# A hint ahead of the general path's branch, weight sums in place over four steps, and separate buffers for the first pair's token sums

## The chip, the cores and the metric

The kernel runs on one core of a Trainium2 chip. Its engines are PE (matrix products; PEld is the loading of weights into it), DVE, ACT and POOL (elementwise work), and SP, which here only issues DMAs. The metric is the time of one execution in device microseconds (us), as the median of three runs: 838.96 us before the change (838.41 to 841.43).

## The reference

```python
for t in range(S):                                  # S = 768, state is 48 x 48 for each of 4 x 8 heads
    kt, vt, rt = (k[:, :, t], v[:, :, t], r[:, :, t])
    cur = np.einsum('bhd,bhe->bhde', u[None] * kt, vt)
    y[:, :, t] = np.einsum('bhd,bhde->bhe', rt, state + cur)
    state = w[None, :, :, None] * state + np.einsum('bhd,bhe->bhde', kt, vt)
x = y.transpose(0, 2, 1, 3).reshape(3072, 384)      # tokens by model width
h = x @ w_in                                        # 384 -> 2048
x = (np.maximum(h, 0.0) + alpha * np.minimum(h, 0.0)) @ w_out   # 2048 -> 384
a, b = x @ w1, x @ w2                               # 384 -> 1024, both
out = (a * b @ w3) @ w_out2                         # 1024 -> 1024 -> 384
```

All is f32 in and out.

## The kernel before

The work runs over six blocks of 128 time steps (all four batches together: 512 tokens). Inside a block the recurrence is done in chunk form for four pairs of heads (a pair is a unit): scores (`sc`, L292), the masked copy of them into `am` (DVE, L305 and L308) and the outputs `py` (L351, L357). The outputs are the `x` of the next block's first layer, so the units of block i+1 and the layer of block i are interleaved. A block's first layer has 16 steps f: `product1` (PE, `ph`, nine matmuls, one of two PSUM banks by the parity of f), `relus` (ACT, L583 and L584), `slope` (DVE, L589), `halves` (ACT and POOL, `gh` and `gl`) and, three steps behind, `down1` (PE, `acc`, nine matmuls). Every f32 product is made of three matmuls on a high and a low half of both operands; `split` makes the halves (ACT casts the high, POOL subtracts for the low).

The second layer multiplies w3 by w_out2 first (`fold`: 24 matmuls into `pf`, for each of eight j), so that its end is one product with `m`. Its two first products are done for two blocks at once, a pair of blocks p = 0, 1, 2, in the seven products of Strassen's form as rearranged here. This wants sums of weights (the **mix**: b = w11-w10, e = b+w01, a = e-w00, p = w01+w11) and sums of tokens (`x_sum`). The second layer's weights were split during the earlier blocks and lie in DRAM (`s12`, `so2`, `s3`).

The order on each engine is that in which the program calls things: a written schedule (`MIDDLE`, a list of words for every four steps, and `LAST` for the last block) names the calls of each step. In the fifth block (i == NB-2) an even step ends with `mix_store` of the former weight slice and `mix_load` of the next, an odd step with `mix`, the sums and the split. All engines are in-order queues, SP too. SP gives each DMA one of eight semaphores in turn, and a DMA waits until the one that had the same semaphore has landed.

In the last block `extra` (the word `xx`) starts what the second layer needs: two `w3` slices at the block's start (`fetch_3`), the weights by step (`fetch_12`), the eight `so2` slices (`fetch_o2`), a `fold` in each of the steps 4 to 11, the loads of `x2d` and the first sums of tokens. Fold j+2's `w3` is loaded right behind fold j, into the two buffers of tags `rk` and `nat`. The first sums of tokens, at steps 6 and 7, take their buffer from the tag `rk` too. The first four `so2` slices use the four buffers of the tag `raw`, which the mix uses as well. The group f of a pair in `second` is 42 matmuls of the seven products with 18 of the output product between them.

At the end stands `tc.If(flag > 0)` over `general()`, the path for weights w out of a range. The data here never take it, so every engine branches over its code (L1128), waits once for its semaphores in the short block behind it, and passes the final barrier (L1209).

## Time and profile before

| | |
|---|---|
| median of three runs | 838.96 us |
| the profiled execution | 837.99 us |
| its span, first to last instruction | 836.2 us |
| mean granted clock of PE | 0.995 of full speed |
| busy PE, DVE, POOL, ACT | 97%, 63%, 51%, 43% |
| DMA traffic | 139.5 MB, 167 GB/s in the mean |

The page gives the busy time of each engine, and the span in 40 slices. A timeline lists instructions in order: start, length, engine, line, operation, output and inputs, sizes, and in brackets the idle time in front of it and what ended that. A q behind an engine's name is its sequencer, which issues DMAs, waits and branches. Waits are summed by waiter and by what it waited for.

### The profile page before, as it was taken

To read this page: it belongs to the slowest core of one execution; us is meant where nothing else is said; L and a number is where in the kernel's file an instruction comes from. 1 tells how busy PE (TensorE), PEld (TensorE's weight loads), DVE (VectorE), ACT (ScalarE), POOL (GpSimd) and SP (SyncE) were. 2 spreads that over 40 slices of the span, in tenths; PEclk is the share of its full clock that TensorE was granted. 3 is DMA by queue.
4 is the path that set the end of the run, shared out by engine and by line. 5 is a ranking of instruction groups with operands and counts; after the bars stand their busy time and mean duration, and the time that the engine had idled before them with its cause. 6 is when DMAs were issued, how large, how long until landed. Compare 5 with 4: busy or idle time off the path is not lost.

```text
span 836.2 us, 13560 instructions
## 1 busy us (share of the span) xinstructions
PE 814.5 (97%) x4910; PEld 669.9 (80%) x4910; DVE 529.6 (63%) x880; ACT 355.7 (43%) x703; POOL 422.6 (51%) x342
## 2 busy tenths in 40 slices
PE   8999999999999999999889999999999999999995
PEld 7777788888888888888778898888887888888884
DVE  5899998988787887766654121154467445674442
ACT  3587666555555565543345232432223222331221
POOL 3778876766677667655654122342244223432221
PEclk9999999999999999999999999999999999999999
DMA  8666765766677677655539735325332453342002
GB/s 251 181 205 188 201 216 163 253 211 236 211 222 229 179 232 197 191 161 154 158 121 313 286 127 205 101 94 185 118 109 100 151 189 114 106 160 76 1 0 81
DMA packets 63247, 139.52 MB, mean 167 GB/s; under 512 B 7169, under 2 KB 24066, under 8 KB 63170
## 3 DMA queue, kind: packets, MB, share of 16 engines
q1 hardware_dynamic: 62338, 137.24, 52.0%
q10 hardware_dynamic: 832, 1.31, 0.5%
q8 instruction: 41, 0.67, 0.3%
q14 instruction: 36, 0.29, 0.1%
HBM read 104.15 MB, written 31.46 MB: 162 GB/s over the span
## 4 chain that ended last, share of the span: by engine, by line
PE 77%; DMA 7%; DVE 5%; issue 3%; POOL 3%; ACT 2%; SPq 2%; DVEq 0%; POOLq 0%; ACTq 0%
PE pq L753 21%; PE acc L124 8%; PE acc L125 7%; PE acc L126 7%; PE ph L124 6%; PE ph L125 6%; PE ph L126 6%; PE py L357 2%; PE py L351 2%; PE acb L126 2%; PE acb L124 2%; PE acb L125 2%; DMA mix<-s 2%; DMA wo<-so 1%; PE pf L125 1%
## 5 line engine op out<-in xcount | busy, mean ns | idle before, releaser
L121 POOL TENSOR_TENSOR gl<-g,gh 128x512 fp32r<-128x512 f32 x96 | 126.5, 1318 | 118.2 <-ACT gh L120 115.2
L121 POOL TENSOR_TENSOR gl<-t,gh 128x512 fp32r<-128x512 f32 x48 | 72.1, 1509 | 169.4 <-PE pq L753 145.3
L764 DVE TENSOR_TENSOR t<-pq,t 128x512 f32<-128x512 f32 x96 | 66.2, 689 | 97.4 <-PE pq L753 97.4
L124 PE MATMUL ph<-x,wi 128*128 128x512 f32 x288 | 115.5, 401 | 4.3 <-ACT p L584 3.1
L589 DVE SCALAR_TENSOR_TENSOR g<-g,keep,p 128x512 f32<-128x512 f32 x80 | 78.6, 983 | 61.5 <-ACT p L584 58.1
L124 PE MATMUL acc<-gh,wo 128*128 128x512 f32 x288 | 114.4, 397 | 0.0
L125 PE MATMUL ph<-x,wi 128*128 128x512 f32 x288 | 113.1, 393 | 1.2 <-POOL wi L150 1.2
L126 PE MATMUL ph<-x,wi 128*128 128x512 f32 x288 | 112.5, 390 | 0.0
L125 PE MATMUL acc<-gh,wo 128*128 128x512 f32 x288 | 112.3, 390 | 0.0
L126 PE MATMUL acc<-gl,wo 128*128 128x512 f32 x288 | 112.3, 390 | 0.0
L753 PE MATMUL pq<-x,w 128*128 128x512 f32 x408 | 110.8, 390 | 0.0
L753 PE MATMUL pq<-xc,w 128*128 128x512 f32 x384 | 107.1, 391 | 0.0
L120 ACT CAST gh<-t 128x512 fp32r<-128x512 f32 x48 | 29.9, 623 | 140.3 <-DVE t L764 140.3
L753 PEld LDWEIGHTS pq<-x,w 128*128 128x128 f32 x408 | 76.6, 188 | 16.1 <-DVE t L764 0.2
L753 PEld LDWEIGHTS pq<-xc,w 128*128 128x128 f32 x384 | 72.0, 188 | 15.8 <-DVE xc L708 0.6
L120 ACT CAST gh<-g 128x512 fp32r<-128x512 f32 x96 | 59.2, 619 | 52.8 <-DVE g L589 51.9
L583 ACT ACTIVATE g<-ph 128x512 f32<-128x512 f32 x96 | 56.9, 593 | 37.4 <-PE ph L126 35.3
L124 PEld LDWEIGHTS ph<-x,wi 128*128 128x128 f32 x288 | 54.1, 188 | 18.7 <-ACT p L584 4.3
L124 PEld LDWEIGHTS acc<-gh,wo 128*128 128x128 f32 x288 | 54.1, 188 | 12.5 <-issue 1.1
L125 PEld LDWEIGHTS ph<-x,wi 128*128 128x128 f32 x288 | 54.1, 188 | 12.4 <-POOL wi L150 2.2
L126 PEld LDWEIGHTS ph<-x,wi 128*128 128x128 f32 x288 | 54.1, 188 | 11.5
L126 PEld LDWEIGHTS acc<-gl,wo 128*128 128x128 f32 x288 | 54.1, 188 | 11.3
(138 smaller groups left out, 1482.8 us busy)
## 6 DMA issues: line engine op xcount, KB each, us to landing
w<-s SPq DMA_DIRECT2D x72, 384.0 KB, 4.4
raw<-in_wA SPq DMA_DIRECT2D x32, 384.0 KB, 3.8
s<-raw SPq DMA_DIRECT2D x32, 384.0 KB, 4.1
nat<-in_nat SPq DMA_DIRECT2D x20, 576.0 KB, 7.1
rk<-in_rkT SPq DMA_DIRECT2D x20, 448.0 KB, 6.5
raw<-in_wB SPq DMA_DIRECT2D x16, 384.0 KB, 5.1
raw<-in_w3T SPq DMA_DIRECT2D x16, 384.0 KB, 4.2
x2d<-o SPq DMA_DIRECT2D x18, 256.0 KB, 2.1
```

The lines of the kernel that those rows point to most:

```text
L120: nc.scalar.copy(out=dst_h, in_=src)
L121: (lo or nc.gpsimd).tensor_tensor(out=dst_l, in0=src, in1=dst_h.bitcast(F32), op=ALU.subtract)
L124: nc.tensor.matmul(out=o, lhsT=wh, rhs=xh, start=first, stop=False)
L125: nc.tensor.matmul(out=o, lhsT=wl, rhs=xh, start=False, stop=False)
L126: nc.tensor.matmul(out=o, lhsT=wh, rhs=xl, start=False, stop=last)
L351: nc.tensor.matmul(out=py[o:e, b], lhsT=state[:, hp, b, o:e], rhs=t["rs"][:, b], start=b == 0, stop=False, skip_group_check=True,)
L357: nc.tensor.matmul(out=py[o:e, b], lhsT=t["v"][:, b, D * j:D * j + e - o], rhs=t["am"][:, B * j + b], start=i == 0 and b == 0, stop=True, ...
L583: nc.scalar.activation(out=g, in_=ph, func=ACTF.Relu, scale=-1.0)
L589: nc.vector.scalar_tensor_tensor(out=g, in0=g, scalar=alpha[:, f:f + 1], in1=p, op0=ALU.mult, op1=ALU.add)
L753: nc.tensor.matmul(out=o, lhsT=u, rhs=v, start=first and n == 0, stop=last and n == 2, skip_group_check=True)
L764: nc.vector.tensor_tensor(out=o, in0=x, in1=y, op=how)
```

## The change

- **The hint.** `second(True)` marks a place ahead of the last group for a branch hint with the label of the branch over `general()`, on all engines.
- **The mix.** The sums are now made in the buffers that the loads filled (two tiles instead of six for a slice): `mix` makes the sums in the first half of each tile, the new `mix_split` puts the high halves into the second and the low ones into the first, and `mix_store` writes them back in six DMAs instead of four. `mix_step` runs the four in four successive steps: load at an even step, sums in the odd one behind it, the split in the even one behind that, the store in the next odd one. The last slice so runs into the first two steps of the last block. In the stored layout b and a change places, and `where` in `group` follows.
- **The `so2` loads.** In the last block slices 4 to 7 are issued ahead of the first `fetch_12`, and slices 0 to 3 at step 2 instead of step 1.
- **The token sums.** The first two sums of the first pair take buffers of the tag `o` in the pool `gp`, not of `rk`.

```diff
--- before.py
+++ after.py
@@ -463,24 +463,32 @@
             nc.sync.dma_start(out=parts[j], in_=seen(f, j, 0, 2))
 
     def mix(f):
-        parts = mixes[f]
-        t, o = (st.tile([P, 4, P], F32, tag="raw", name="mix") for _ in range(2))
         op = nc.vector.tensor_tensor
-        for j in range(2):
-            op(out=t[:, 2 * j:2 * j + 2], in0=parts[j][:, 0], in1=parts[j][:, 1], op=ALU.add)
-        w00, w01, w10, w11 = (t[:, m] for m in range(4))
-        op(out=o[:, 0], in0=w11, in1=w10, op=ALU.subtract)
-        op(out=o[:, 1], in0=o[:, 0], in1=w01, op=ALU.add)
-        op(out=o[:, 2], in0=o[:, 1], in1=w00, op=ALU.subtract)
-        op(out=o[:, 3], in0=w01, in1=w11, op=ALU.add)
-        mixes[f] = h, l = [st.tile([P, 4, P], F32R, tag="raw", name="mix") for _ in range(2)]
-        split(h, l, o)
+        for x in mixes[f]:
+            op(out=x[:, 0], in0=x[:, 0], in1=x[:, 1], op=ALU.add)
+        (w00, w01), (w10, w11) = ((x[:, 0, 0], x[:, 0, 1]) for x in mixes[f])
+        op(out=w10, in0=w11, in1=w10, op=ALU.subtract)
+        op(out=w11, in0=w11, in1=w01, op=ALU.add)
+        op(out=w01, in0=w10, in1=w01, op=ALU.add)
+        op(out=w00, in0=w01, in1=w00, op=ALU.subtract)
+
+    def mix_split(f):
+        for x in mixes[f]:
+            nc.scalar.copy(out=x[:, 1].bitcast(F32R), in_=x[:, 0])
+            nc.gpsimd.tensor_tensor(out=x[:, 0].bitcast(F32R), in0=x[:, 0], in1=x[:, 1], op=ALU.subtract)
 
     def mix_store(f):
-        for s, x in enumerate(mixes.pop(f)):
-            x = x.bitcast(F32)
-            nc.sync.dma_start(out=seen(f, 2, 0, KD)[:, s], in_=x[:, 0:KD])
-            nc.sync.dma_start(out=seen(f, 1, 1, 2)[:, s], in_=x[:, KD:])
+        ae, bp = mixes.pop(f)
+        for s in range(2):
+            nc.sync.dma_start(out=seen(f, 2, 0, 2)[:, s], in_=ae[:, 1 - s])
+            nc.sync.dma_start(out=seen(f, 2, 2, 3)[:, s], in_=bp[:, 1 - s, 0:1])
+            nc.sync.dma_start(out=seen(f, 1, 1, 2)[:, s], in_=bp[:, 1 - s, 1:2])
+
+    def mix_step(k):
+        for fn, n in ((mix_store, 3), (mix_split, 2), (mix, 1), (mix_load, 0)):
+            f, odd = divmod(k - n, 2)
+            if not odd and 0 <= f < M2:
+                fn(f)
 
     def fetch_o2(k):
         if k < 5:
@@ -683,10 +691,12 @@
 
     def x_sum(p, name):
         k = NAMES.index(name)
-        if k in (1, 3, 5):
-            xt2[p, k] = ld.tile([P, 2, N], F32, tag="rk", name="xsum")
-        s = xt2[p, k] if k in (1, 3, 5) else xt2[p, k - 1]
-        s = s[:, k in (2, 4)]
+        if p == 0 and k < 3:
+            s = gp.tile([P, N], F32, tag="o", name="xsum", bufs=3)
+        else:
+            if k in (1, 3, 5):
+                xt2[p, k] = ld.tile([P, 2, N], F32, tag="rk", name="xsum")
+            s = (xt2[p, k] if k in (1, 3, 5) else xt2[p, k - 1])[:, k in (2, 4)]
         xs[p, name, "sum"] = s
         if name[0] == "-":
             nc.vector.scalar_tensor_tensor(
@@ -743,7 +753,7 @@
 
     def group(p, f, after):
         w = [w2s[3 * (M2 * p + f) + m] for m in range(3)]
-        where = {"w00": (0, 0), "w01": (0, 1), "w02": (0, 2), "w10": (1, 0), "p": (1, 1), "w12": (1, 2), "b": (2, 0), "e": (2, 1), "a": (2, 2)}
+        where = {"w00": (0, 0), "w01": (0, 1), "w02": (0, 2), "w10": (1, 0), "p": (1, 1), "w12": (1, 2), "a": (2, 0), "e": (2, 1), "b": (2, 2)}
 
         def times(o, name, x, first, last=True):
             m, c = where[name]
@@ -822,7 +832,7 @@
         after(8)
         pull()
 
-    def second():
+    def second(hint=False):
         for k in range(NB // 2 * M2):
             p, f = divmod(k, M2)
 
@@ -856,6 +866,8 @@
                             x_low(p + 1, "x21", nc.vector)
                             x_cast(p + 1, "x20")
 
+            if hint and k == NB // 2 * M2 - 1:
+                tc.mark_branch_hint_location("rare", engines=mybir.ALL_ENGINES)
             if f == 3 and p + 1 < NB // 2:
                 load_x2(p + 1)
             group(p, f, after)
@@ -1045,11 +1057,9 @@
 
         def extra(x):
             f = x % M1
-            if f == 0:
-                mix_store(M2 - 1)
+            for k in {0: (4, 5, 6, 7), 2: (0, 1, 2, 3)}.get(f, ()):
+                fetch_o2(k)
             fetch_12(f)
-            for k in ((4, 5, 6, 7), (0, 1, 2, 3))[f] if f < 2 else ():
-                fetch_o2(k)
             if f == 2:
                 late[0] = True
             j = f - 4
@@ -1109,13 +1119,8 @@
                         table[name](x - k)
                 else:
                     table[name](x)
-            if i == NB - 2:
-                if f % 2:
-                    mix(f // 2)
-                else:
-                    if f:
-                        mix_store(f // 2 - 1)
-                    mix_load(f // 2)
+            if i >= NB - 2:
+                mix_step(x - M1 * (NB - 2))
         if STOP:
             return
         table["hl"](NB * M1 - 1)
@@ -1123,9 +1128,9 @@
             for c in range(KD):
                 queue.append(lambda f=f, c=c: down(NB - 1, f, wo[f], M1, x2d, (c,)))
         pull()
-        second()
+        second(True)
     flag = nc.values_load(rare, min_val=0, max_val=1)
-    with tc.If(flag > 0):
+    with tc.If(flag > 0, label="rare"):
         general()
```

How this moves instructions: on ACT in the fifth block (steps 4 to 7 of it; `gh` is the cast of a step's product, `g` and `p` its two relus, `x` the outputs of a unit). Before:

```order
L120 CAST gh<-g 128x512
L583 ACTIVATE g<-ph 128x512
L584 ACTIVATE p<-ph 128x512
L120 CAST mix<-mix 128x512
L120 CAST gh<-g 128x512
L394 CAST x<-py 112x512
L583 ACTIVATE g<-ph 128x512
L584 ACTIVATE p<-ph 128x512
L120 CAST gh<-g 128x512
L583 ACTIVATE g<-ph 128x512
L584 ACTIVATE p<-ph 128x512
```

and now:

```order
L477 CAST mix<-mix 128x256 x2
L120 CAST gh<-g 128x512
L591 ACTIVATE g<-ph 128x512
L592 ACTIVATE p<-ph 128x512
L120 CAST gh<-g 128x512
L394 CAST x<-py 112x512
L591 ACTIVATE g<-ph 128x512
L592 ACTIVATE p<-ph 128x512
L477 CAST mix<-mix 128x256 x2
L120 CAST gh<-g 128x512
L591 ACTIVATE g<-ph 128x512
```

The cast of the mix stood in front of a step's casts and relus, directly behind the sums; now its two halves stand behind the relus of a step in which the sums are a step old.

On SP at the same place (`x<-e` moves a unit's outputs and waits for them, `mix<-s` is the load of the next slice, `s<-mix` the store; `rk` and `nat` are the inputs of a later unit). Before:

```order
L366 DMA x<-e 16x2x512 x2
L482 DMA s_108<-mix 128x384
L483 DMA s_108<-mix 128x128
L482 DMA s_108<-mix 128x384
L483 DMA s_108<-mix 128x128
L463 DMA mix<-s_108 128x2x256 x2
L173 DMA rk<-in_rkT 112x1024
L174 DMA nat<-in_nat 128x1152
```

and now:

```order
L366 DMA x<-e 16x2x512 x2
L463 DMA mix<-s_108 128x2x256 x2
L483 DMA s_108<-mix 128x256
L484 DMA s_108<-mix 128x128
L485 DMA s_108<-mix 128x128
L483 DMA s_108<-mix 128x256
L484 DMA s_108<-mix 128x128
L485 DMA s_108<-mix 128x128
L173 DMA rk<-in_rkT 112x1024
L174 DMA nat<-in_nat 128x1152
```

The load stood behind four stores of the slice before; now it stands ahead of them, right behind the move of the outputs.

On SP in the steps 1 to 2 of the last block (`wo<-so` are `so2` slices, `x2d<-o` the first layer's results of the fifth block, `w` the weights of the second layer). Before:

```order
L453 DMA w_1_5220<-s_108 128x768
L488 DMA wo_5222<-so_109 128x768
L488 DMA wo_5224<-so_109 128x768
L488 DMA wo_5226<-so_109 128x768
L488 DMA wo_5228<-so_109 128x768
L626 DMA x2d<-o 128x512 x3
L453 DMA w_2_5267<-s_108 128x768
```

and now:

```order
L453 DMA w_1_5214<-s_108 128x768
L483 DMA s_108<-mix 128x256
L484 DMA s_108<-mix 128x128
L485 DMA s_108<-mix 128x128
L483 DMA s_108<-mix 128x256
L484 DMA s_108<-mix 128x128
L485 DMA s_108<-mix 128x128
L634 DMA x2d<-o 128x512 x3
L496 DMA wo_5259<-so_109 128x768
L496 DMA wo_5261<-so_109 128x768
L496 DMA wo_5263<-so_109 128x768
L496 DMA wo_5265<-so_109 128x768
L453 DMA w_2_5267<-s_108 128x768
```

The four `so2` slices 0 to 3 now stand behind the last stores of the mix and the three stores of results.

The hint, on SP, at the top of the program (PE, ACT, DVE and POOL have it as the first instruction behind the branch into the kernel as well):

```order
L1214 UNCONDITIONAL_BRANCH
L1214 BRANCH_PREFETCH_HINT
L1003 DMA wu<-in_wu 112x8
L1017 DMA brief<-in_brief 128x256
L1017 DMA in_128<-in_rkT 112x512
L1017 DMA nat<-in_nat 128x384
```

It is not ahead of the last group, but ahead of the whole program: it has no operands that would hold it at its place.

## Rows read from the trace of the kernel before

**Rows 1.** The page: busy time of each engine over the whole span

```profile
PE 814.5 (97%) x4910; PEld 669.9 (80%) x4910; DVE 529.6 (63%) x880; ACT 355.7 (43%) x703; POOL 422.6 (51%) x342
```

**Rows 2.** PE timeline (start, length, work, [idle before <-releaser]): blocks' py work, one stall

```profile
368.77 1.09 PE L351 MATMUL py<-rs,state 112*64 112x128 f32 x16
...
388.28 1.09 PE L351 MATMUL py<-rs,state 112*64 112x128 f32 x16
...
407.66 0.50 PE L124 MATMUL ph<-x,wi 128*128 128x512 f32 x1 [1.67 <-ACT p L584]
...
410.63 1.08 PE L351 MATMUL py<-rs,state 112*64 112x128 f32 x16 [0.63 <-DVE am L308]
...
432.61 1.08 PE L351 MATMUL py<-rs,state 112*64 112x128 f32 x16 [0.64 <-DVE am L308]
```

**Rows 3.** DVE timeline: the first sum of the mix before the stall at 407

```profile
402.75 0.43 DVE L470 TENSOR_TENSOR mix<-mix 128x256 f32<-128x256 f32 x1 [2.11 <-DMA mix<-s]
```

**Rows 4.** ACT timeline: the cast of the mix before the same stall

```profile
405.49 0.62 ACT L120 CAST mix<-mix 128x512 fp32r<-128x512 f32 x1 [6.19 <-DVE mix L475]
```

**Rows 5.** Waits from 374 to 440 us (waiter <- waited for: us, times, longest)

```profile
ACT mix L120 <- DVE mix L475: 30.9, 6, 6.2
POOL mix L121 <- ACT mix L120: 19.1, 4, 6.3
```

**Rows 6.** SP timeline (DMA issues): store and load of the mix

```profile
397.57 0.58 SPq L482 DMA_DIRECT2D s<-mix  x1
...
399.66 1.23 SPq L463 DMA_DIRECT2D mix<-s  x2
```

**Rows 7.** ACT timeline: casts of four successive folds

```profile
491.00 0.48 ACT L120 CAST m<-pf 128x384 fp32r<-128x384 f32 x1 [5.07 <-PE pf L126]
...
499.31 0.48 ACT L120 CAST m<-pf 128x384 fp32r<-128x384 f32 x1 [5.07 <-PE pf L126]
...
508.24 0.48 ACT L120 CAST m<-pf 128x384 fp32r<-128x384 f32 x1 [5.70 <-PE pf L126]
...
517.87 0.48 ACT L120 CAST m<-pf 128x384 fp32r<-128x384 f32 x1 [6.39 <-PE pf L126]
```

**Rows 8.** SP timeline: the first of two held w3 loads

```profile
499.31 0.32 SPq L503 DMA_DIRECT2D w3h<-s  x1
```

**Rows 9.** PE timeline: last block before the first fold, the fold, the product after it

```profile
457.07 0.39 PE L124 MATMUL ph<-x,wi 128*128 128x512 f32 x1
...
461.15 0.34 PE L124 MATMUL pf<-wo,w3h 128*128 128x384 f32 x1
...
465.88 0.40 PE L124 MATMUL ph<-x,wi 128*128 128x512 f32 x1
```

**Rows 10.** SP timeline: first issues of the last block

```profile
442.08 0.60 SPq L503 DMA_DIRECT2D w3l<-s  x1
446.17 0.32 SPq L482 DMA_DIRECT2D s<-mix  x1
...
454.70 1.97 SPq L488 DMA_DIRECT2D wo<-so  x4
456.77 1.66 SPq L626 DMA_DIRECT2D x2d<-o  x3
```

**Rows 11.** ACT timeline, last row: the last output's issue

```profile
828.01 0.38 ACTq L738 DMA_DIRECT2D out<-o  x1
```

**Rows 12.** DMA issues from 820 us on (KB each, us to landing)

```profile
out<-o ACTq DMA_DIRECT2D x1, 256.0 KB, 3.8
```

**Rows 13.** The branch line 1128 on SP (ns min/median/max, first and last start)

```profile
L1128 SPq EVENT_SEMAPHORE  x8: 17/17/17, 832.5 to 834.8; - x8
...
L1128 SPq COMPARE_BRANCH  x1: 45/45/45, 828.3 to 828.3; - x1
```

**Rows 14.** Waits of SP's queue from 820 us on

```profile
SPq L1128 <- SPq L1128: 5.9, 2, 4.1
```

**Rows 15.** The page: code loads of PE (packets, MB, share)

```profile
q8 instruction: 41, 0.67, 0.3%
```

## The prediction

> **What bounds the kernel now.** I read the page's busy times first: PE is busy for 814.5 of 836.2 us [rows 1]. Any gain must therefore come from the some 20 us in which PE stands or the program runs without it, so I next looked in PE's timeline for idle times above 0.2 us, then at who ended each, and last at what SP does after PE's end. Three places matter to this change.
>
> First, the fifth block. PE's work on `py` comes once in four steps; from 368.77 to 388.28 that took 19.51 us, from there to 410.63 it took 22.35, and to 432.61 it took 21.98 [rows 2]. So two periods in which the mix runs are 2.84 and 2.47 us too long, 5.31 us together. The rows show two stalls in such a period: 1.67 us before a product that waits for ACT's relu of line 584, and 0.63 before `py`, which waits for DVE's masked copy. ACT's cast of the mix, just ahead of that relu in its queue, sat 6.19 us for DVE's sums [rows 4], and DVE sat 2.11 us for the load of the mix [rows 3]. Summed over the stretch ACT's cast waited 30.9 us in six times [rows 5]. The load is late because SP issues it at 399.66, behind stores from 397.57 on [rows 6]. So data that only the second layer uses holds the queues of two engines that the first layer needs now.
>
> Second, the folds. The casts behind successive folds stand 8.31 us apart, then 8.93, then 9.63 [rows 7]: two folds lose 0.62 and 1.32 us, 1.94 together. Their `w3` came late: the first held load is issued at 499.31, when the fold before ends [rows 7, 8], although the buffer pair turns after two folds. The tag `rk` has two buffers and the first token sums take a third turn of it (line 687 of the code), so a load waits for one fold more. The same happens once more after it. A smaller stall is in the very first fold: it runs from 461.15 to 465.88, 4.73 us [rows 9], where 8.31 less the 4.08 of a step's 18 other matmuls (457.07 to 461.15) gives 4.23. It loses 0.50 us, and its late input is `so2`, issued at 454.70 [rows 10].
>
> Third, the tail. The last output is issued at 828.01 and needs 3.8 us, so it lands at 831.8 [rows 11, 12]. SP branches over the general path at 828.3, yet its eight waits behind the branch run from 832.5 to 834.8 [rows 13]. The waits of SP on itself are 5.9 us in two pieces, the longer 4.1 [rows 14]: 4.1 us behind the branch and 1.8 in the midst of the eight waits. Neither ends with a semaphore of another engine; this is code that is not there yet.
>
> **The change part by part.** The sum is made against the profiled execution, 837.99 us (span 836.2 and 1.8 around it), 0.97 below the median of the three runs; I carry the saving over to the median.
>
> *Mix.* The sums keep their place on DVE, but the load moves ahead of the stores: 397.57 instead of 399.66, 2.09 us earlier [rows 6], which covers DVE's 2.11 us wait [rows 3] but for 0.02. DVE's queue behind the wait (the diagonal `am`, the slope, the masked copy) moves up as much. Independently, ACT's cast leaves its place between the sums and the relu. It now finds sums a step old, so its 6.19 us wait goes and nothing behind it is late. The full-width cast takes 0.62 us [rows 4]; two of half width cost between 0.62 and 1.24 together, over eight slices at most 5.0 us more, on an engine that stood 30.9 us in this stretch [rows 5]. POOL's low half becomes two instructions as well, behind the unit's `q`; at most twice the time of before, and POOL stood 19.1 us for ACT's casts [rows 5]. The product of a step uses its `gl` two steps later, which hides the shift. SP issues 16 more stores; four took 2.09 us [rows 6], so 16 take 8.4 us, spread over eight slices. They stand ahead of the inputs of a later unit, and these are not waited for soon. A load also waits until the stores two slices older have landed, whose issue is now up to a step before it; what is queued behind it on SP are the stores, whose data nobody awaits. What would be late next on PE in this block is PE itself. Value: 5.31 saved. Bounds: 0 saved if the load comes as late as before and DVE carries the whole delay to PE, 5.31 if both stalls go.
>
> *Token sums.* They leave `rk`, so a `w3` load waits for the fold two back and has a whole fold period of 8.31 us [rows 7] where it had about half. Value 1.94 saved; bounds 0 and 1.94. Their new buffers were last used by the results stored at 456.77 [rows 10], long before.
>
> *`so2`.* Slices 0 to 3 wait for the buffers of the last mix stores and queue behind those and the three result stores. In favour: SP now does not stand from 442.08 + 0.60 to 446.17 before the last slice's stores [rows 10], 3.5 us in which slices 4 to 7 can be issued. Against: the results' stores, issued at 456.77 in 1.66 us [rows 10], come first now, so if nothing else moves the slices go out at 458.43 instead of 454.70, 3.7 us later, all of it on PE's path as that fold already waits. Bounds: 0.5 saved (the stall of before goes) to 3.7 lost. I take 0.5 lost, nearer to the good end, as ACT, which copies those results, is behind by the mix's waits before and no longer now, and the queue gets 3.5 us back.
>
> *Hint.* The hint stands at the program's start on every engine, not where the source puts it. If it lasts until the branch, SP's waits end with the landing at 831.8; the eight waits without their inner 1.8 us take 2.3 - 1.8 = 0.5, and from 834.8 to the end at 836.2 are 1.4: 833.7 instead of 836.2, 2.5 saved. Landing and waking cost a little, so I take 2.4. The other engines' branches lie beside the last DMA. Bounds: 2.5 saved; 0 if it does nothing; and a loss of 4.1 [rows 14] for each code load that it spoils on PE's path. [...] No row here shows a hint at work.
>
> Sum: 5.31 + 1.94 + 2.4 - 0.5 = 9.15 us. 837.99 becomes 828.84, and the median 838.96 becomes 829.8.
>
> **Rivals.**
> *The `so2` slices are the new stall.* The first fold waits 3.7 us more instead of 0.5: 829.8 + 3.2 = 833.0. For it: the order on SP, and DMAs issued there at 454.70 met a fold at 461.15 that still waited. Against: the freed 3.5 us.
> *The hint does nothing*, since it is hundreds of instructions early: 829.8 + 2.4 = 832.2. SP's code also moves by some 17 rows, so the inner 1.8 us can go by itself, and then it is 830.4. For it: the place. Against: the instruction names the branch that it belongs to, so nothing in it has to run out before that.
> *The mix's wait stays on DVE.* If the load lands as late as before (its buffers now come free by stores), PE's masked copy and relu stay late: 829.8 + 5.3 = 835.1, no change that can be told. Against: the 2.09 us, and ACT's relu is free in any case.
> *Slower: the hint spoils code loading.* If from the program's start on the hint replaces the load of the next block of code by that of the branch's target, PE stands at each of its block ends. A stand is 4.1 us as on SP [rows 14]; the third such stand eats the 9.15 us, and all 41 code loads of PE [rows 15] would be 168 us, near 1000. For it: only the hint's place. Against: a hint that names one branch has no reason to change the loads far ahead of it, and PE now shows no wait for any of its code loads, so they run with time to spare.
>
> **How the numbers follow.** Forecast 0.62 at 829.8, in its own range from 828.8 (the old fold stall goes too) to 831. The `so2` stall 0.13 at 833.0; no effect of the hint 0.13 at 832.2; the mix's wait 0.08 at 835.1; slower 0.04. Less than 0.5%, 4.2 us, is no change by what the runs can tell. Faster so needs less than 834.8: 0.62 + 0.13 + 0.13 = 0.88; the same 0.08; slower 0.04. The range goes from 828.4 to 834.2, which leaves out the last two cases.
>
> **What the new profile would show.** `py` periods of 19.5 us throughout the fifth block, and no wait of ACT's new cast for the sums; fold casts 8.31 us apart with no idle time of PE before a `w3` half; SP's wait for itself behind the branch gone and the span's end about 2 us behind the last landing. Wrong would be: a fold at step 4 that lasts over 5.2 us, code loads that PE waits for, or a period that stays over 21 us.

## The result: 840.19 us before, 830.04 us after

| | before | after |
|---|---|---|
| median (runs, lowest to highest) | 840.19 us (4; 838.41 to 841.59) | 830.04 us (4; 829.4 to 832.28) |
| ratio, 95% interval | | 0.9885 (0.9855 to 0.9915) |
| profiled execution, its span | 837.99, 836.2 us | 829.9, 828.1 us |
| sixteenth `py` (L351) of the program begins at | 348.93 us | 350.47 us |
| from there to the span's end | 487.27 us | 477.63 us |
| of it the three periods of `py` from 368.77 and 370.31 | 63.84 us | 58.53 us |
| of it from PE's last end to the span's end | 8.84 us | 6.89 us |

The change touches nothing ahead of the sixteenth `py` but the hint at the program's start, and what the program needs until there differs between the profiled executions by over 6 us (348.86 to 355.19 in the table of the experiments; seven of them, of programs alike up to there, lie between 349.12 and 355.19). So the stretch from the sixteenth `py` to the end is the measure used below: 9.64 us less in this pair of profiles, of which the `py` periods give 5.31, the stretch from the first fold to the eighth 2.03 (60.66 to 58.63), the tail 1.95, and the products behind the last fold 0.36, a term that nothing in the prediction names. The span's end is printed to 0.1 us, so the rest and the tail of any kernel can be off by 0.05.

The page of the changed kernel, busy times and the code loads of its queues (packets, MB, share); PE's 814.5 us of [rows 1] are 813.5 of a shorter span, and PE's code loads are one fewer than in [rows 15]:

```profile
PE 813.5 (98%) x4910; PEld 670.8 (81%) x4910; DVE 537.9 (65%) x880; ACT 357.9 (43%) x711; POOL 427.0 (52%) x350
...
q8 instruction: 40, 0.66, 0.4%
q14 instruction: 32, 0.25, 0.1%
```

PE's timeline, the four beginnings of `py` that answer to [rows 2]:

```profile
370.31 1.09 PE L351 MATMUL py<-rs,state 112*64 112x128 f32 x16
...
389.82 1.09 PE L351 MATMUL py<-rs,state 112*64 112x128 f32 x16
...
409.33 1.09 PE L351 MATMUL py<-rs,state 112*64 112x128 f32 x16
...
428.85 1.09 PE L351 MATMUL py<-rs,state 112*64 112x128 f32 x16
```

They stand 19.51 us apart each time, and no idle time is noted in front of any. The waits of the mix in the same stretch (waiter <- waited for: us, times, longest), against [rows 5]:

```profile
ACT mix L477 <- DVE mix L473: 12.3, 5, 3.4
POOL mix L478 <- ACT mix L477: 12.0, 6, 2.6
...
DVE mix L468 <- DMA s<-mix: 1.5, 1, 1.5
DVE mix L468 <- DMA mix<-s: 1.2, 3, 0.6
```

ACT's cast still waits for the sums, 12.3 us in place of 30.9. The later step does not take the wait away, as the prediction had it; it lets it end in time. ACT's timeline, the casts behind the last four folds, against [rows 7]:

```profile
495.48 0.48 ACT L120 CAST m<-pf 128x384 fp32r<-128x384 f32 x1 [5.07 <-PE pf L126]
...
503.79 0.48 ACT L120 CAST m<-pf 128x384 fp32r<-128x384 f32 x1 [5.07 <-PE pf L126]
...
512.09 0.48 ACT L120 CAST m<-pf 128x384 fp32r<-128x384 f32 x1 [5.07 <-PE pf L126]
...
520.40 0.48 ACT L120 CAST m<-pf 128x384 fp32r<-128x384 f32 x1 [5.07 <-PE pf L126]
```

All 8.31 us apart. SP at the tail: its last issue but one in the timeline, then by line (ns min/median/max, first and last start) the eight waits behind the branch and the branch, against [rows 13]:

```profile
820.50 1.81 SPq L748 DMA_DIRECT2D out<-o  x1
...
L1133 SPq EVENT_SEMAPHORE  x8: 17/17/17, 826.2 to 826.7; - x8
...
L1133 SPq COMPARE_BRANCH  x1: 73/73/73, 822.8 to 822.8; - x1
```

The eight waits run from 826.2 to 826.7 with no stop inside. They begin when the last output lands (826.17), and from there to the span's end are 1.9 us, where it was 4.4 before (831.8 to 836.2). But that output was late: SP's issue at 820.50 took 1.81 us, where most of its output issues take 0.33 to 0.34, and the one behind it came only at 822.40. The waits of SP's queue on itself, against the 5.9 us in two pieces of [rows 14], are one wait for that landing:

```profile
SPq L1133 <- SPq L1133: 3.3, 1, 3.3
```

### The profile page after: what moved, and what is told of

It is laid out like the page before. It is cut to its first block, busy times and chain, and to the rows that moved or that the text cites. A ratio compares the mean times of both kernels' runs of the same rounds, so it can differ in the third digit from the quotient of the medians.

```text
span 828.1 us, 13628 instructions
## 1 busy us (share of the span) xinstructions
PE 813.5 (98%) x4910; PEld 670.8 (81%) x4910; DVE 537.9 (65%) x880; ACT 357.9 (43%) x711; POOL 427.0 (52%) x350
## 4 chain that ended last, share of the span: by engine, by line
PE 86%; DMA 4%; DVE 3%; issue 2%; POOL 2%; ACT 1%; SPq 1%; DVEq 0%; POOLq 0%; ACTq 0%
PE pq L763 21%; PE acc L124 9%; PE acc L126 9%; PE acc L125 9%; PE ph L124 7%; PE ph L125 7%; PE ph L126 7%; PE py L357 2%; PE py L351 2%; PE acb L126 2%; PE acb L124 2%; PE acb L125 2%; PE sc L292 2%; DMA wo<-so 1%; PE pf L124 1%
## 5 line engine op out<-in xcount | busy, mean ns | idle before, releaser
L597 DVE SCALAR_TENSOR_TENSOR g<-g,keep,p 128x512 f32<-128x512 f32 x80 | 74.1, 926 | 65.4 <-ACT p L592 64.4
```

What stands on the lines that cost most here:

```text
L597: nc.vector.scalar_tensor_tensor(out=g, in0=g, scalar=alpha[:, f:f + 1], in1=p, op0=ALU.mult, op1=ALU.add)
```

## The experiments

All were timed beside the kernel before on the same chip; "rest" is the time from the sixteenth `py` to the end of the profiled execution's span, and "tail" the part of it behind PE's last end.

| kernel | median, us | ratio to before (95%) | sixteenth `py` | rest | last two `py` periods | first fold to second | tail |
|---|---|---|---|---|---|---|---|
| before | | | 348.93 | 487.27 | 22.35, 21.98 | 8.86 | 8.84 |
| after | 830.04 | 0.9885 (0.9855 to 0.9915) | 350.47 | 477.63 | 19.51, 19.51 | 8.77 | 6.89 |
| after, again | 832.55 | 0.9928 (0.9902 to 0.9955) | 349.93 | 479.47 | 19.51, 19.51 | 10.09 | 6.90 |
| before with the hint alone | 839.30 | 0.9986 (0.9965 to 1.0006) | 348.86 | 483.94 | 21.91, 21.77 | 8.36 | 6.11 |
| after without the hint | 830.53 | 0.9883 (0.9858 to 0.9907) | 350.65 | 477.35 | 19.51, 19.51 | 8.97 | 6.39 |
| before, SP's code shifted | 839.06 | 0.9976 (0.9962 to 0.9990) | 351.10 | 486.40 | 23.13, 21.94 | 8.33 | 7.36 |
| after, hint not on PE | 833.82 | 0.9917 (0.9901 to 0.9932) | 354.64 | 477.26 | 19.51, 19.51 | 8.70 | 6.60 |
| after, split early | 832.45 | 0.9911 (0.9886 to 0.9937) | 349.12 | 478.49 | 19.76, 20.30 | 8.72 | 6.78 |
| after, stores ahead of the load | 839.14 | 0.9973 (0.9951 to 0.9996) | 355.19 | 486.71 | 22.08, 23.64 | 8.51 | 6.82 |
| after, load a step later | 843.26 | 1.0036 (1.0017 to 1.0056) | 352.08 | 491.12 | 23.54, 22.59 | 11.03 | 6.80 |
| after, `so2` a step later | 833.80 | 0.9912 (0.9887 to 0.9937) | 355.07 | 478.53 | 19.51, 19.51 | 9.55 | 6.75 |
| after, sums back in `rk` | 836.02 | 0.9961 (0.9946 to 0.9977) | 353.77 | 480.43 | 19.51, 19.51 | 10.09 | 6.38 |
| after, 12 idle products | 832.38 | 0.9919 (0.9902 to 0.9936) | 351.86 | 478.54 | 19.51, 19.51 | 10.09 | 6.47 |
| after, 10 idle products | 831.21 | 0.9916 (0.9896 to 0.9937) | 350.66 | 478.64 | 19.51, 19.51 | 9.73 | 6.89 |

### The hint

Before with the hint alone (`mark_branch_hint_location` and the label, as in the change's diff):

> The kernel before with the hint and its label alone. Theory: SP's waits behind the branch start when the last output lands, with no inner stop of 1.8 us; PE's last end to the span's end goes from 8.84 to between 6.4 and 7.0 us, and the time falls by 1.8 to 2.5 us, unless the start loses as the changed kernel's did (then by 0.3 to 1 us). Rival (the hint does nothing, the code's shift did it): the tail stays at 8.8 us, or falls by the inner 1.8 us with the 4.1 us behind the branch still there.

By line, SP's waits behind the branch, and the branch:

```profile
L1130 SPq EVENT_SEMAPHORE  x8: 17/17/17, 830.3 to 831.4; - x8
...
L1130 SPq COMPARE_BRANCH  x1: 70/70/70, 827.4 to 827.4; - x1
```

The branch and the first wait behind it on ACT, and the branch on PE's queue, in the kernel before and then with the hint alone:

```profile
L1128 PEldq COMPARE_BRANCH  x1: 3922/3922/3922, 825.3 to 825.3; - x1
...
L1128 ACTq COMPARE_BRANCH  x1: 54/54/54, 829.2 to 829.2; - x1
...
L1128 ACTq EVENT_SEMAPHORE  x1: 17/17/17, 832.2 to 832.2; - x1
```

```profile
L1130 PEldq COMPARE_BRANCH  x1: 408/408/408, 824.6 to 824.6; - x1
...
L1130 ACTq COMPARE_BRANCH  x1: 68/68/68, 828.6 to 828.6; - x1
...
L1130 ACTq EVENT_SEMAPHORE  x1: 17/17/17, 829.1 to 829.1; - x1
```

So the hint is at work at the branch. PE's branch takes 0.4 us in place of 3.9, and ACT stands 0.5 us behind its branch in place of 3.0. All eleven profiles with the hint on ACT have its stand at 0.50 us, and the three without it at 2.9 to 4.3.

The tail is 6.11 us, 2.73 less. The first wait ends at 830.35, 0.02 us behind the landing of the DMA that it is for (830.33), the second at 830.94 with the last landing (830.92), and the stop inside is gone. On SP itself the rows do not show when it was ready, since its first wait ends with a landing; the kernel with SP's code shifted, below, has the same 0.02 us without a hint. Of the 2.73 us the quicker landing of the last output makes 0.2 (3.6 us in place of 3.8). The median shows 1.05 us, with an interval that holds no change.

After without the hint:

```diff
-        second(True)
+        second()
```

> The changed kernel without the hint instruction, all else kept. Theory (the hint makes the code behind the branch present in time): SP's waits behind its branch start again some 4 us after the branch, and the time from PE's last end to the span's end goes from 6.9 us back to between 8.3 and 8.9 us; the time rises by 1.4 to 2.0 us to about 831.5 to 832. Rival (the shift of SP's code alone removed the inner 1.8 us, the hint does nothing): PE's end to span's end stays at 6.9 to 7.1 us and the time stays within 0.3 us. On the 1.54 us that the changed kernel loses at the start (half clock of PE for 6.83 us in place of 3.41): if the hint makes it, PE's first py comes at about 51.5 us again instead of 53.0; if it is chance or other code, 53.0 stays or it falls either way.

The issue that took 1.81 us, and SP's rows at the branch:

```profile
820.89 0.33 SPq L748 DMA_DIRECT2D out<-o  x1
...
L1133 SPq EVENT_SEMAPHORE  x8: 17/17/17, 825.5 to 826.3; - x8
...
L1133 SPq COMPARE_BRANCH  x1: 53/53/53, 822.3 to 822.3; - x1
```

The theory falls: the tail gets shorter, 6.39 us. SP stands behind its branch as before, from 822.33 to 825.50, 3.1 us, but the last output lands only at 825.89, so the stand costs nothing; and the stop in the eight waits does not come back. The issue takes 0.33 us. From the last landing to the span's end are 2.1 us, 0.2 more than with the hint. What removed the 1.8 us in the changed kernel is thus not the hint, or not it alone.

Before with eight of the last block's weight loads split in two, which moves SP's code, without hint:

```diff
-        nc.sync.dma_start(out=x.bitcast(F32).rearrange("p s c m -> p (s c m)"), in_=s12[q % SLOTS])
+        y = x.bitcast(F32).rearrange("p s c m -> p (s c m)")
+        for h in range(1 + (8 <= q < M1)):
+            w = 2 * KD * P // (1 + (8 <= q < M1))
+            nc.sync.dma_start(out=y[:, h * w:h * w + w], in_=s12[q % SLOTS][:, h * w:h * w + w])
```

> The kernel before, without hint, with eight of the weight loads of the last block split into two DMAs each, so that SP has 8 more instructions ahead of its branch and 16 more ahead of the block behind it (with eight more on the path not taken). Theory (the stop of 1.8 us in the midst of the eight waits is the end of a block of SP's code, which then lies ahead of these waits): the eight waits run through in 0.5 to 0.9 us, the stand behind the branch (3.2 to 4.1 us) ends about when the last output lands, and from PE's end to the span's end are 6.3 to 7.0 us in place of 8.84: 1.8 to 2.5 us faster with no hint. Rival (only the hint removes it): the tail stays at 8.5 to 8.9 us.

```profile
829.44 1.61 SPq L741 DMA_DIRECT2D out<-o  x1
...
L1131 SPq EVENT_SEMAPHORE  x8: 17/17/17, 835.5 to 836.1; - x8
...
L1131 SPq COMPARE_BRANCH  x1: 45/45/45, 831.6 to 831.6; - x1
```

The eight waits run through in 0.6 us, and the first ends with the last landing (835.51): the stop goes without a hint, with the place of SP's code. The tail is 7.36 and not 6.3 to 7.0, since here, too, an issue of SP was held, 1.61 us.

That hold is ascribed to PE's code: each time, a 16 KB packet of the code queue q8 is under way. (That q8 is PE's is seen from its packets, 41 without the hint, 40 with it, and 41 again when PE alone is left without it, below.) The packet's start and end beside the issues that met it:

| kernel | PE's last code load ahead of its end | SP issue that met it |
|---|---|---|
| before | 826.58 to 827.90 | 826.65, 0.33 us; 827.43, 0.86 us |
| after | 820.24 to 821.94 | 820.50, 1.81 us |
| after without the hint | 820.79 to 821.88 | 820.89, 0.33 us; 821.68, 0.59 us |
| before with the hint alone | 825.90 to 827.01 | 825.98, 0.33 us; 826.77, 0.55 us |
| before, code shifted | 829.33 to 830.75 | 829.44, 1.61 us |

But for those of 0.33 us, each issue ends 0.3 to 0.4 us behind the load. The same holds beyond these rows, and so do the exceptions. In the fourteen profiles 54 of SP's issues begin inside such a load and take over 0.7 us, and 52 of them end 0.28 to 0.42 us behind it. But of all 232 that begin inside one, 108 end before it does, most of them after 0.32 to 0.34 us. Of the 40 that came into a load behind another issue 34 were held so, of the 192 that came first 54. What decides it stays open. With the hint on all engines but PE:

```diff
-                tc.mark_branch_hint_location("rare", engines=mybir.ALL_ENGINES)
+                tc.mark_branch_hint_location("rare", engines=[e for e in mybir.ALL_ENGINES if e != mybir.EngineType.PE])
```

> The changed kernel with the hint on all engines but PE. In the changed kernel SP's last DMA issue but one took 1.81 us (820.50 to 822.31) while a 16 KB load of PE's code (820.24 to 821.94) ran; without any hint that load started 0.82 us ahead of PE's last end in place of 0.97, and the same issue took 0.33. Theory (PE's own hint instruction shifts PE's code by one, so that its last load starts in front of SP's issue and holds it): here the load starts 0.8 us ahead of PE's end, the issue takes 0.33 us, and from PE's end to the span's end are 6.4 us in place of 6.9; the time falls by 0.5 us against the changed kernel, less than its runs spread. Rival (SP's own hint holds SP ahead of its branch): the issue still takes 1.5 to 1.8 us and the tail stays at 6.9.

PE's branch, with no hint on PE again, took 4.2 us (from 823.2; 0.4 with the hint on PE), and ACT's stand stayed at 0.5, so with the other engines hinted PE's branch was as long as without any hint (3.9). PE's last load ahead of its end came at 825.06, 0.24 us ahead of it; the issue at 824.59 took 0.33 us and the next, at 825.38, 0.98. The tail is 6.60. So SP's own hint does not hold SP, which was the rival; the long issue again ends 0.38 us behind a load of PE's code. That PE's hint sets the start of that load is not shown: without it the load came 0.82 us ahead of PE's end in one kernel and 0.24 in the other.

### The mix

Split in the step of the sums, as before the change, the load ahead of the stores:

```diff
-        for fn, n in ((mix_store, 3), (mix_split, 2), (mix, 1), (mix_load, 0)):
+        for fn, n in ((mix_store, 3), (mix, 1), (mix_split, 1), (mix_load, 0)):
```

> The changed kernel with ACT's and POOL's split of the mixed weights put back right behind DVE's sums in the same step; the load keeps its place ahead of the stores, sums in place as in the change. Theory (what cost 5.31 us was ACT's cast that waits for DVE's sums ahead of the relus): ACT's cast waits 3 us or more again in each slice, py periods go up to 21 to 22.4 us in most of the fifth block, and 3 to 5.3 us of the saving are lost: about 833 to 835 us. Rival (the earlier load was what helped, as the prediction's working puts it first): py periods stay within 0.3 us of 19.51 and the time within 0.5 us of the changed kernel.

The largest stall of PE in the block, and ACT's cast in the waits:

```profile
428.52 1.08 PE L351 MATMUL py<-rs,state 112*64 112x128 f32 x16 [0.55 <-DVE am L308]
```

```profile
ACT mix L477 <- DVE mix L473: 26.5, 6, 5.0
```

ACT's cast waits nearly as long in all as before the change, 30.9 us then, and yet only 1.04 us of the 5.31 come back (periods of 19.76 and 20.30); PE's idle time is all ahead of `py` (0.17 and 0.55), none ahead of the products that wait for the relus. Neither side of the expectation had this size: with the cast in its old place the early load, with the sums in place and the stores as changed, brings 4.27 us. Next, stores of a slice a step later and ahead of the next load:

```diff
-        for fn, n in ((mix_store, 3), (mix_split, 2), (mix, 1), (mix_load, 0)):
+        for fn, n in ((mix_store, 4), (mix_store, 3), (mix_split, 2), (mix, 1), (mix_load, 0)):
             f, odd = divmod(k - n, 2)
-            if not odd and 0 <= f < M2:
+            if not odd and 0 <= f < M2 and (fn is not mix_store or (f < M2 - 2) == (n == 4)):
```

> The changed kernel with the stores of a mixed slice one step later, ahead of the load of the next slice but one in the same step (slices 0 to 5; the last two as in the change), so that the load of the mix is late again, by two to three us or more; the split keeps its own step. Theory (the cast's place is what matters): DVE's sums wait 2 to 5 us for the load, but py periods stay below 20 us; at most 1 us lost. Rival (the load ahead of the stores is what removed the stalls): DVE carries the wait to the masked copy and the slope, py periods of 20.5 to 22 us, 2 to 5 us lost: 832 to 835 us.

```profile
416.61 1.08 PE L351 MATMUL py<-rs,state 112*64 112x128 f32 x16 [2.50 <-DVE am L308]
```

The stalls are back, 2.50 us here and 4.04 one period on, all ahead of `py`, and 6.70 us of the periods are lost, with 2.7 more ahead of the first fold: the rival, and more than it said. Since there the load also waits until the stores beside it have landed, the last kernel keeps the stores where the change has them and moves the load behind them:

```diff
-        for fn, n in ((mix_store, 3), (mix_split, 2), (mix, 1), (mix_load, 0)):
+        for fn, n in ((mix_store, 3), (mix_load, 1), (mix, 1), (mix_split, 2)):
```

> The changed kernel with the load of the mix one step later on SP, behind the six stores of the former slice, so that it is about as late against PE as in the kernel before (some 3 us later than in the changed kernel); ACT's and POOL's split keeps its own step behind the sums. Theory A (the early load did most; the kernel with the early load and the cast in its old place lost 1.04 of the 5.31 us): DVE's sums wait 2 to 3 us for the load again, PE's stalls are all ahead of py and none ahead of the products that wait for the relus; two or three py periods of 20.5 to 22 us, 3 to 5 us lost. Theory B (the cast's place alone would do too): py periods below 20.2 us, at most 1.3 us lost, the part of the old stalls that stood ahead of py (0.63 and 0.64 us).

PE's two stalls, and DVE's sums ahead of the first of them:

```profile
414.97 1.95 PE L351 MATMUL py<-rs,state 112*64 112x128 f32 x16 [3.96 <-DVE am L308]
...
437.56 1.08 PE L351 MATMUL py<-rs,state 112*64 112x128 f32 x16 [1.52 <-DVE am L308]
```

```profile
407.45 0.42 DVE L468 TENSOR_TENSOR mix<-mix 128x256 f32<-128x256 f32 x1 [3.25 <-DMA mix<-s]
409.86 0.42 DVE L468 TENSOR_TENSOR mix<-mix 128x256 f32<-128x256 f32 x1 [1.98 <-DMA mix<-s]
```

Theory A, and beyond its numbers: 7.11 us in the periods (4.03 and 3.08) and 6.5 more until the second fold. DVE sits 3.25 and 1.98 us for the load (2.11 in [rows 3]) and hands it to `am`, ahead of `py`. The load is issued 4.45 us behind the `x<-e` ahead of it on SP (404.46 against 400.01), where it was 3.47 before the change (399.66 against 396.19) and is 1.43 in it (397.57 against 396.14); so this kernel is some 1 us later than before, and it loses more than before did.

What ties these kernels together is when DVE ends the sums of the slice whose load stands behind `x<-e` on SP, counted from the `py` that begins the period. The last of these sums in the first period, before and after the change, whose `py` begin at 388.28 and 389.82:

```profile
405.17 0.28 DVE L475 TENSOR_TENSOR mix<-mix 128x128 f32<-128x128 f32 x1
```

```profile
403.97 0.29 DVE L473 TENSOR_TENSOR mix<-mix 128x128 f32<-128x128 f32 x1
```

| kernel | cast of the mix | sums end behind `py`, us | period over 19.51, us | end less excess, us |
|---|---|---|---|---|
| before | behind the sums | 17.18, 16.81 | 2.84, 2.47 | 14.34, 14.34 |
| after, split early | behind the sums | 14.40, 14.94 | 0.25, 0.79 | 14.15, 14.15 |
| after | a step later | 14.44, 15.19 | 0, 0 | |
| after, stores ahead of the load | a step later | 18.69, 20.25 | 2.57, 4.13 | 16.12, 16.12 |
| after, load a step later | a step later | 20.15, 19.20 | 4.03, 3.08 | 16.12, 16.12 |

So a period has a deadline for the sums, and each microsecond behind it is lost. The early load brings their end forward by 2.7 and 1.6 us; the cast's later place moves the deadline back by 1.8 us, from 14.3 to 16.1. An estimate from these numbers for the cast's place without the early load is 17.18 and 16.81 less 16.12, 1.1 and 0.7 us lost: 3.6 of the 5.31 us saved. The load alone saves 4.27. The two overlap, and no kernel here has the cast's place with the sums just as late as before.

### The last block

Sums back in `rk`:

```diff
-        if p == 0 and k < 3:
+        if p < 0:
```

> The changed kernel with the first two token sums back in the buffers of rk, all else as changed. Theory: the casts behind the folds stand 8.31 us apart but for two, 8.9 and 9.6, and PE waits for the high half of w3 at these two: 1.94 us from the sixteenth py to the span's end above the changed kernel's 477.6. Rival (the other edits already moved the loads of w3 early enough): all 8.31 apart and nothing lost.

ACT's casts behind the folds, and PE's stalls:

```profile
491.80 0.48 ACT L120 CAST m<-pf 128x384 fp32r<-128x384 f32 x1 [5.07 <-PE pf L126]
...
500.11 0.48 ACT L120 CAST m<-pf 128x384 fp32r<-128x384 f32 x1 [5.07 <-PE pf L126]
...
509.01 0.48 ACT L120 CAST m<-pf 128x384 fp32r<-128x384 f32 x1 [5.66 <-PE pf L126]
...
518.66 0.48 ACT L120 CAST m<-pf 128x384 fp32r<-128x384 f32 x1 [6.42 <-PE pf L126]
```

```profile
504.70 0.44 PE L125 MATMUL pf<-wo,w3l 128*128 128x384 f32 x1 [0.33 <-DMA w3l<-s]
...
514.35 0.44 PE L125 MATMUL pf<-wo,w3l 128*128 128x384 f32 x1 [0.77 <-DMA w3l<-s]
```

The casts stand 8.31, 8.90 and 9.65 us apart: 0.59 and 1.34, 1.93 us. (PE waits for the low half of `w3`, not the high one as expected.) The `so2` slices 0 to 3 a step later:

```diff
-            for k in {0: (4, 5, 6, 7), 2: (0, 1, 2, 3)}.get(f, ()):
+            for k in {0: (4, 5, 6, 7), 3: (0, 1, 2, 3)}.get(f, ()):
```

> The changed kernel with the so2 slices 0 to 3 one step later still (step 3 of the last block in place of step 2). This prices the rival of the prediction in which these slices stall the first fold. In the changed kernel they are issued at 451.87 and the first fold runs from 457.42 to 461.88. Theory (no slack beyond a step): issued some 4.9 us later, the slices land at 460 to 462 and the first fold takes 3 to 5 us longer; 3 to 5 us lost, all other folds 8.31 apart. Rival (there is slack, the slices wait for something else that a step doesn't move): the first fold takes less than 1 us longer.

The first fold takes 0.78 us longer, no more: the rival. Even that need not be the step's, since the second of the four issues (457.86) took 1.34 us beside a load of PE's code (457.87 to 458.83). The `so2` edit was not taken back by itself. A step later in the code moves these issues past one weight load only, which on SP takes about 0.5 us (three take 1.38 us in the changed kernel, from 455.05 on), since SP runs ahead of the engines there; the step of a call is not its time.

The changed kernel once more, on the chip of the kernel with the sums back in `rk` and of the two with more idle products:

> The changed kernel once more, word for word, beside the two kernels with more idle products, so that they are compared on one chip. Expected: from the sixteenth py (L351) to the span's end 477.6 us as in its first profile (477.63; the kernel before 487.27), whatever the start takes; the time anywhere from 829 to 836 us, with the start: sixteenth py between 349 and 355 us.

Its rest is 479.47, not 477.6, and all of the difference lies at the first fold (10.09 to the second, 8.77 in the first profile; and 0.5 us just ahead of it). PE's stalls in that fold, and SP's first of the four `so2` issues:

```profile
457.37 0.41 PE L124 MATMUL pf<-wo,w3h 128*128 128x384 f32 x1 [0.34 <-DMA wo<-so]
...
459.24 0.45 PE L124 MATMUL pf<-wo,w3h 128*128 128x384 f32 x1 [0.26 <-DMA wo<-so]
...
460.61 0.44 PE L124 MATMUL pf<-wo,w3h 128*128 128x384 f32 x1 [0.57 <-DMA wo<-so]
```

```profile
451.54 2.33 SPq L496 DMA_DIRECT2D wo<-so  x1
```

SP's issue took 2.33 us, with PE's code load from 451.72 to 453.51 beside it; in the first profile it was the third of the four (452.87, 1.67 us, beside a load from 452.83 to 454.17). Which issue is held goes with what the first fold takes. With a hold at the first or second of the four, or just ahead of them, it is 9.55 to 10.09 us to the second fold (five kernels, four of them on this chip); with one at the third 8.77 and 8.72 (after; split early); with none 8.97, 8.70 and 8.51 (without the hint; hint not on PE; stores ahead of the load). The kernel with the load a step later stands apart, as its first fold waits 4.02 us in one piece. This is the rival of the prediction, the slices as the new stall, with another cause than the order on SP. Whether the chip or chance sets the meeting is not shown.

### The start

In `STARTUP`, and with `wm10` in the second of the two:

```diff
-ks1 ks3 pw0 ks0 rs0 ld4 wm8 S0 kk0 q0 red0 rs1 am0 rs2 U0 q1 S1 red1 q2 am1 fill0 Y0 q3 fill1 wm1 Y1 rs3 S3 car0
+ks1 ks3 pw0 ks0 rs0 ld4 wm12 S0 kk0 q0 red0 rs1 am0 rs2 U0 q1 S1 red1 q2 am1 fill0 Y0 q3 fill1 wm1 Y1 rs3 S3 car0
```

> The changed kernel with 12 in place of 8 idle products of PE ahead of the first scores (four more, 0.45 us each, so PE works until about 15.7 us instead of 13.9). In the profiles so far the first scores wait 0.4 to 3.1 us for the first inputs in seven kernels, and PE's granted clock is then at half for 6.8 us and more. Theory (PE's idle time ahead of the scores brings the half clock and with it the lost time): the clock stays full until some 19 us also where the inputs are late, the sixteenth py comes at 349 to 351 us, and the time is 1 to 4 us below that of the changed kernel on the same chip if its starts are late there. Rival (the half clock comes from what stands later, or the idle products only delay): the sixteenth py comes at 350.5 to 356 us as before, and the time is the same or up to 1.8 us longer.

> As the one with 12, but with 10 idle products, so PE works until about 14.8 us. Theory: waits of the first scores of under 0.9 us bring no half clock ahead of 19 us any more, longer ones do; the time between that of the changed kernel and that with 12. Rival: no difference from the changed kernel beyond the 0.9 us of the two products.

Medians of 832.38 and 831.21 us against 832.55 of the unchanged kernel on that chip: no difference that the spread of 3 to 7 us lets see. Stretches of the start in the unchanged kernel and then in the one with 12 idle products (start and end, length, busy us and instructions of PE, PEld, DVE, ACT and POOL, then PE's granted clock, DMA share, GB/s):

```profile
12.00:16.00 4.00, 2.42 (x20) 1.86 (x20) 3.56 (x4) 0.58 (x2) 2.39 (x3) 1.00 1.08 274
16.00:20.00 4.00, 4.00 (x59) 3.67 (x55) 3.20 (x5) 2.45 (x9) 0.00 (x0) 1.00 1.00 327
20.00:24.00 4.00, 2.93 (x29) 1.93 (x30) 2.69 (x5) 3.97 (x13) 3.79 (x4) 1.00 0.28 68
24.00:28.00 4.00, 4.00 (x40) 3.22 (x36) 2.93 (x6) 0.11 (x1) 2.86 (x3) 1.00 0.69 226
```

```profile
12.00:16.00 4.00, 4.00 (x21) 3.26 (x19) 4.00 (x5) 0.58 (x2) 2.08 (x2) 1.00 1.08 312
16.00:20.00 4.00, 4.00 (x60) 3.69 (x60) 2.37 (x4) 1.87 (x7) 0.00 (x0) 1.00 0.79 258
20.00:24.00 4.00, 3.84 (x23) 3.00 (x23) 2.32 (x4) 3.89 (x14) 3.06 (x3) 0.54 0.00 0
24.00:28.00 4.00, 4.00 (x35) 2.97 (x34) 3.65 (x8) 0.84 (x2) 3.59 (x4) 0.61 0.80 256
```

The unchanged kernel waited 1.58 us for its first scores and kept the full clock (1.00 in all four stretches); the one with 12 idle products kept PE at work until 16 us and had the half clock for most of 20 to 24 (0.54 of full speed in the mean). The theory falls. Its ground was wrong too: of the kernels profiled until then six, not seven, had waited for their first scores, and the one with the load a step later, which waited 2.17 us, kept the full clock until 42 us. What decides when the clock falls there stays open. That it has to do with the change is not shown: the changed kernel reached the sixteenth `py` at 350.47 and 349.93, two kernels without the mix's change at 348.86 and 351.10.

## Why the prediction was right

It forecast 829.8 us and a saving of 9.15; the first profile saves 9.64 from the sixteenth `py` on, the second 7.80. That the median came within 0.24 us of the forecast is luck in part: two terms were right to 0.01 us, and the errors of the others went both ways.

- *Mix*, 5.31 forecast, 5.31 measured, by the two causes that the working gave, which overlap: 4.27 us by the early load without the cast's move (split early), and the last 1.04 with it. Three things in the step were off. ACT's cast "finds sums a step old, so its 6.19 us wait goes"; it still waits 12.3 us in all, up to 3.4 at once, and "no wait of ACT's new cast for the sums" did not come true. The load was to cover DVE's wait "but for 0.02"; in fact DVE still waits 0.25 and 1.53 us at 400 to 403, and PE does not see it. And the bound, "0 saved if the load comes as late as before", was wrong on both sides: by the deadlines above 3.6 us would still be saved (an estimate), and with the load 1 us later than before, the two periods were 1.8 us longer than before the change (46.13 against 44.33).
- *Token sums*, 1.94 forecast; 1.94 by the casts of the change, 1.93 lost when undone.
- *`so2`*, 0.5 lost forecast; 0.09 saved (8.86 to 8.77) in one profile and 1.23 lost (10.09) in the other. The stretch forecast, 0.5 saved to 3.7 lost, holds both. Less the 4.08 us of a step's other matmuls the fold took 4.69 and 6.01 us, so the prediction's own sign of being wrong, a fold over 5.2, stands in the second profile. The order on SP did not bring it: a step more costs 0.78 at most. It goes with whether, and at which of these issues, a load of PE's code is met, which the prediction did not see.
- *Hint*, 2.4 forecast, 1.95 measured at the tail. The sum of the step was right: from the last landing to the span's end it is 4.4 us before and 1.9 now, 2.4 to 2.5 saved, and some 0.5 was lost as the landing came later behind PE's end, with the issue that was held. The cause was not: in the changed kernel without the hint the same stretch is 2.1 us and the tail 0.5 us shorter, and with SP's code shifted, no hint, the stretch is 2.0. The inner 1.8 us went with the place of SP's code, which the prediction had only in a rival ("can go by itself"), and SP's stand behind the branch is hidden by the last landing. Where the stop exists, in the kernel before, the hint takes away 2.73 us. What the hint changed is measured in the kernel before with the hint alone: ACT stands 0.5 us behind its branch in place of 3.0, and q14 has 31 code loads in place of 36. Behind the prediction's reading of SP's two pieces, code that is not there yet, stand the shift of SP's code, with which the inner one went, and the code loads of q14 inside both in the profile before (four from 828.3 to 832.5, two from 832.6 to 834.6); whose they are, no row says.
- The *slower rival*, code loads spoiled on PE's path, is excluded: no idle time of PE over 0.1 us is without a releaser, and PE has 40 loads in place of 41. The one that is gone stood behind PE's end (830.46 in the profile before).

What the sum left out is the start, which moved 1.54 us against the change in the first profile; it scatters by more than that among programs with the same start. The median came out at 830.04 on one chip and 832.55 on another; over the ten runs of the changed kernel it is 831.3.

No kernel here beats the changed one clear of the noise. Dropping the hint keeps its whole gain (0.9883 against 0.9885), so in these runs the hint is worth its line only as cover against the place of the code.

## What to carry to other kernels

Ask of a late input which queue it stands behind before asking who waits for it: moving one load ahead of the stores saved 4.27 of 5.31 us with the cast, which then waited 26.5 us, left in its place. That wait's length was no cost here; its end against the next deadline was, with 1.04 us lost. And before crediting a hint or a barrier with what a new trace no longer shows, undo it alone: a shift of SP's code by 16 instructions removed the same stop.

## What the runs showed of the hardware that was not expected

Some DMA issues on SP that fell into a 16 KB load of PE's code ended 0.3 to 0.4 us behind the load's end: they took 1.81 (after), 1.61 (before, code shifted), 0.98 (after, hint not on PE) and 2.33 us (after, again) in place of 0.33 to 0.45. It is no rule for every issue: of 232 that began inside such a load in the fourteen profiles 88 ended so, and 108 were done before the load was. The same meeting goes with the first fold's stall: to the second fold 9.55 to 10.09 us in the five kernels with a held issue at the first or second of the four `so2` slices or just ahead of them, 8.51 to 8.97 in the three with none.

With a branch hint at the program's start, in the kernel before with the hint alone, PE's branch at 824.6 us took 0.4 us in place of 3.9, and ACT's stand behind its own 0.5 in place of 3.0.

SP's eight waits stopped for 1.8 us in their midst in the one profile of the kernel before, and in none of the kernels whose code ahead of them had grown by 16 rows or more or that carried the hint.
